# Rewriting a linear-attention and mixture-of-experts kernel: decay before the transposes, state in PSUM, small matmuls for the sums, one load queue, a fixed order

One core of one Trainium2 chip. The metric is the time of one execution in device microseconds (us); lower is better. A slow run is over 1.5% above the fastest of its kernel; comparisons below use fast runs.

## The reference, cut to what matters

```python
# attention, per batch b (4) and head h (8), head size 48, 768 steps
for t in range(S):
    cur = einsum('bhd,bhe->bhde', u * kt, vt)
    y[:, :, t] = einsum('bhd,bhde->bhe', rt, state + cur)
    state = w * state + einsum('bhd,bhe->bhde', kt, vt)
# mixture of experts, one expert per batch (sentence)
e_idx = argmax(x.mean(axis=1) @ w_gate)          # x: (4, 768, 384)
out[b] = gate[b] * (relu(x[b] @ w1[e]) @ w2[e])  # w1 (8, 384, 1024), w2 (8, 1024, 384)
```

The kernels cut each batch into 6 chunks of 128 steps, so there are 24 chunks. Inside a chunk the recurrence becomes masked matmuls; between chunks a state is carried. An expert can be chosen only when its batch's six chunks are done, so the expert of batch b runs beside the chunks of batch b+1, and the last one runs alone.

## The kernel before

```python
    # loads of one chunk (r, k in f32 by SyncE; v cast to bf16 by a POOL-issued transfer)
    nc.sync.dma_start(out=rr32[:, :, 0:D], in_=r[b, :, s0 : s0 + C, :].transpose([1, 0, 2]))
    nc.sync.dma_start(out=kk32[:, :, 0:D], in_=k[b, :, s0 : s0 + C, :].transpose([1, 0, 2]))
    nc.gpsimd.dma_start(out=vv, in_=v[b, :, s0 : s0 + C, :].transpose([1, 0, 2]))
    nc.gpsimd.memset(rr32[:, :, D:DP], 0.0)
    nc.gpsimd.memset(kk32[:, :, D:DP], 0.0)
    nc.scalar.copy(rr, rr32)
    nc.scalar.copy(kk, kk32)
    # one chunk
    nc.gpsimd.tensor_mul(ku, kk[:, :, 0:D], u_bc)           # bonus
    nc.gpsimd.tensor_mul(rku, rr[:, :, 0:D], ku)
    nc.vector.reduce_sum(tcol, rku, axis=AX.X)
    nc.gpsimd.tensor_mul(kr, kk, wr)                        # decay for the state
    # ... 8 transposes into PSUM twp ...
    nc.vector.tensor_mul(tw, twp, dcT)                      # decay after the transposes
    # ... scores into atp, twice:
    nc.vector.tensor_mul(gt[:, 4 * wave : 4 * wave + 4, :], atp, maskT)
    # ... y matmuls; 8 state matmuls into kvp ...
    nc.gpsimd.tensor_mul(stmp[0:D], st[0:D, :, 0:D], wCst[0:D])
    nc.gpsimd.tensor_mul(stmp[64 : 64 + D], st[64 : 64 + D, :, D:96], wCst[64 : 64 + D])
    nc.vector.tensor_add(st[0:D, :, 0:D], stmp[0:D], kvp[0:D, :, 0:D])
    # ... and the other half ...
    nc.gpsimd.tensor_mul(vt, vv, tcol.to_broadcast([128, H, D]))
    nc.vector.tensor_add(xn, vt, yp)
    # ... transposes back; eviction with a running sum for the gate ...
```

Of the kernel before, what the change touches and what calls it, by code (L numbers as in the profile page):

```python
# [18 lines left out]
def kernel(  # L19
# [26 lines left out]
    NST = S // 128  # L46

    const = ctx.enter_context(tc.tile_pool(name="const", bufs=1))
    work = ctx.enter_context(tc.tile_pool(name="work", bufs=3))
    inpool = ctx.enter_context(tc.tile_pool(name="inpool", bufs=6))  # L50
    trans = ctx.enter_context(tc.tile_pool(name="trans", bufs=2))
    xpool = ctx.enter_context(tc.tile_pool(name="xpool", bufs=2))
    spool = ctx.enter_context(tc.tile_pool(name="spool", bufs=2))
    wpool = ctx.enter_context(tc.tile_pool(name="wpool", bufs=2))
    hpool = ctx.enter_context(tc.tile_pool(name="hpool", bufs=1))
    opool = ctx.enter_context(tc.tile_pool(name="opool", bufs=3))
    gpool = ctx.enter_context(tc.tile_pool(name="gpool", bufs=2))

    pp_tw = ctx.enter_context(tc.tile_pool(name="pp_tw", bufs=1, space=bass.MemoryType.PSUM))
    pp_at = ctx.enter_context(tc.tile_pool(name="pp_at", bufs=2, space=bass.MemoryType.PSUM))  # L60
    pp_y = ctx.enter_context(tc.tile_pool(name="pp_y", bufs=2, space=bass.MemoryType.PSUM))
    pp_kv = ctx.enter_context(tc.tile_pool(name="pp_kv", bufs=1, space=bass.MemoryType.PSUM))
    pp_moe = ctx.enter_context(tc.tile_pool(name="pp_moe", bufs=2, space=bass.MemoryType.PSUM))

    ident = const.tile([128, 128], BF16, tag="ident", name="ident")
# [4 lines left out]
    )  # L70

# [7 lines left out]
    w_flat = w.rearrange("h d -> (h d)")  # L79
    u_flat = u.rearrange("h d -> (h d)")  # L80
    wbc = const.tile([128, H, D], FP32, tag="wbc", name="wbc")
    nc.sync.dma_start(out=wbc, in_=w_flat.partition_broadcast(128))
    lnw = const.tile([128, H, D], FP32, tag="lnw", name="lnw")
    nc.scalar.activation(out=lnw, in_=wbc, func=ACT.Ln)

    u_bc = const.tile([128, H, D], BF16, tag="u_bc", name="u_bc")
    nc.gpsimd.dma_start(out=u_bc, in_=u_flat.partition_broadcast(128))

    idx_col = const.tile([128, 1], FP32, tag="idx_col", name="idx_col")
    nc.gpsimd.iota(idx_col, pattern=[[0, 1]], base=0, channel_multiplier=1,  # L90
                   allow_small_or_imprecise_dtypes=True)
    idxr_col = const.tile([128, 1], FP32, tag="idxr_col", name="idxr_col")
    nc.gpsimd.iota(idxr_col, pattern=[[0, 1]], base=C - 1, channel_multiplier=-1,
                   allow_small_or_imprecise_dtypes=True)

    scratch = const.tile([128, H, D], FP32, tag="scratch", name="scratch")

    wr = const.tile([128, H, DP], BF16, tag="wr", name="wr")
    nc.vector.memset(wr, 0.0)
    nc.vector.tensor_scalar_mul(scratch, in0=lnw, scalar1=idxr_col[:, 0:1])  # L100
    nc.scalar.activation(out=wr[:, :, 0:D], in_=scratch, func=ACT.Exp)

    wTcol = const.tile([128, NP], FP32, tag="wTcol", name="wTcol")
    nc.vector.memset(wTcol, 1.0)
    for p in range(NP):
        nc.sync.dma_start(out=wTcol[0:D, p : p + 1], in_=w[2 * p, :].rearrange("d -> d ()"))
        nc.sync.dma_start(out=wTcol[64 : 64 + D, p : p + 1], in_=w[2 * p + 1, :].rearrange("d -> d ()"))
    lnwT = const.tile([128, NP], FP32, tag="lnwT", name="lnwT")
    nc.scalar.activation(out=lnwT, in_=wTcol, func=ACT.Ln)

    iota_row = const.tile([128, 128], FP32, tag="iota_row", name="iota_row")
    nc.gpsimd.iota(iota_row, pattern=[[1, 128]], base=0, channel_multiplier=0,
                   allow_small_or_imprecise_dtypes=True)

    dcT = const.tile([128, 2 * NP, 128], BF16, tag="dcT", name="dcT")
    nc.vector.memset(dcT, 0.0)
    scrT = const.tile([128, 128], FP32, tag="scrT", name="scrT")
    for p in range(NP):
        nc.vector.tensor_scalar_mul(scrT, in0=iota_row, scalar1=lnwT[:, p : p + 1])
        for lo, hi in ((0, D), (64, 64 + D)):  # L120
            nc.scalar.activation(out=dcT[lo:hi, p, :], in_=scrT[lo:hi], func=ACT.Exp)
        nc.vector.tensor_scalar(
            out=scrT, in0=iota_row, scalar1=lnwT[:, p : p + 1], scalar2=lnwT[:, p : p + 1],
            op0=ALU.mult, op1=ALU.add,
        )
        for lo, hi in ((0, D), (64, 64 + D)):
            nc.scalar.activation(out=dcT[lo:hi, NP + p, :], in_=scrT[lo:hi], func=ACT.Exp, scale=-1.0)

    wCst = const.tile([128, NP, D], BF16, tag="wCst", name="wCst")
    nc.vector.memset(wCst, 0.0)  # L130
    scrC = const.tile([128, NP], FP32, tag="scrC", name="scrC")
    nc.scalar.activation(out=scrC, in_=lnwT, func=ACT.Exp, scale=float(C))
    nc.vector.tensor_copy(wCst, scrC.to_broadcast([128, NP, D]))

    wg = const.tile([128, NCT, E], FP32, tag="wg", name="wg")
    nc.sync.dma_start(out=wg, in_=moe_w_gate.rearrange("(ct p) e -> p ct e", p=128))
    nc.scalar.mul(wg, wg, 1.0 / float(S))

    ones_row = const.tile([1, 128], FP32, tag="ones_row", name="ones_row")
    nc.vector.memset(ones_row, 1.0)  # L140

    def alloc_batch_tiles(b):
        xt = xpool.tile([128, NCT, S], BF16, tag="xt", name=f"xt{b}")
        st = spool.tile([128, NP, 96], BF16, tag="st", name=f"st{b}")
        nc.vector.memset(st, 0.0)
        pooled_acc = spool.tile([128, NCT], FP32, tag="pooled_acc", name=f"pooled_acc{b}")
        nc.vector.memset(pooled_acc, 0.0)
        return xt, st, pooled_acc

    def load_chunk(b, ci):  # L150
        s0 = ci * C
        rr32 = inpool.tile([128, H, DP], FP32, tag="rr32", name="rr32")
        kk32 = inpool.tile([128, H, DP], FP32, tag="kk32", name="kk32")
        vv = inpool.tile([128, H, D], BF16, tag="vv", name="vv")
        nc.sync.dma_start(out=rr32[:, :, 0:D], in_=r[b, :, s0 : s0 + C, :].transpose([1, 0, 2]))
        nc.sync.dma_start(out=kk32[:, :, 0:D], in_=k[b, :, s0 : s0 + C, :].transpose([1, 0, 2]))
        nc.gpsimd.dma_start(out=vv, in_=v[b, :, s0 : s0 + C, :].transpose([1, 0, 2]))  # L157
        nc.gpsimd.memset(rr32[:, :, D:DP], 0.0)  # L158
        nc.gpsimd.memset(kk32[:, :, D:DP], 0.0)
        rr = inpool.tile([128, H, DP], BF16, tag="rr", name="rr")  # L160
        kk = inpool.tile([128, H, DP], BF16, tag="kk", name="kk")
        nc.scalar.copy(rr, rr32)  # L162
        nc.scalar.copy(kk, kk32)  # L163
        return rr, kk, vv

    def rwkv_chunk(b, ci, xt, st, pooled_acc, loaded):
        s0 = ci * C
        first = ci == 0
        last = ci == NCH - 1
        rr, kk, vv = loaded  # L170

        ku = work.tile([128, H, D], BF16, tag="ku", name="ku")
        rku = work.tile([128, H, D], BF16, tag="rku", name="rku")
        tcol = work.tile([128, H], BF16, tag="tcol", name="tcol")
        nc.gpsimd.tensor_mul(ku, kk[:, :, 0:D], u_bc)  # L175
        nc.gpsimd.tensor_mul(rku, rr[:, :, 0:D], ku)  # L176
        with nc.allow_low_precision("bonus coefficients are small"):
            nc.vector.reduce_sum(tcol, rku, axis=AX.X)  # L178
        kr = work.tile([128, H, DP], BF16, tag="kr", name="kr")
        nc.gpsimd.tensor_mul(kr, kk, wr)  # L180

        twp = pp_tw.tile([128, 2 * NP, 128], BF16, tag="tw", name="twp")
        for p in range(NP):
            nc.tensor.transpose(  # L184
                out=twp[:, p, :],
                in_=rr[:, 2 * p : 2 * p + 2, :].rearrange("s a b -> s (a b)"),
                identity=ident,
            )
            nc.tensor.transpose(  # L189
                out=twp[:, NP + p, :],  # L190
                in_=kk[:, 2 * p : 2 * p + 2, :].rearrange("s a b -> s (a b)"),
                identity=ident,
            )
        tw = trans.tile([128, 2 * NP, 128], BF16, tag="tw", name="tw")
        nc.vector.tensor_mul(tw, twp, dcT)  # L195

        gt = trans.tile([128, H, 128], BF16, tag="gt", name="gt")
# [148 lines left out]
    def emit_moe_jobs(n):  # L346
        for _ in range(n):
            if moe_jobs:
                moe_jobs.pop(0)()
# [76 lines left out]
```

## Time and profile before

| | before |
|---|---|
| median of 3 runs | 227.76 us (227.17 to 228.2) |
| busy: PE, DVE, ACT, POOL | 141.0, 113.1, 92.6, 170.9 us |
| loads of r, k (SyncE), v (POOL), 192 bytes a piece | 4.1, 3.9, 4.1 us from issue to landing |

The engines: PE is TensorE (PEld its weight loads), DVE VectorE, ACT ScalarE, POOL GpSimd, SP SyncE. The page's summary of the chain that ended last, followed back from the last instruction, gives shares of the span by engine:

```profile
POOL 41%; PE 20%; DMA 12%; issue 10%; DVE 8%; ACT 4%; SPq 2%; POOLq 1%; ACTq 0%; DVEq 0%
```

POOL holds most of that chain.

### The profile page before, as it was taken

How to read it: one execution, taken by the hardware profiler on the slowest of the kernel's cores; microseconds unless marked ns; L12 is line 12 of the kernel's file. 1: busy time of each engine (PE TensorE's matmuls, PEld its weight loads, DVE VectorE, ACT ScalarE, POOL GpSimd, SP SyncE). 2: the span in 40 equal slices, each digit the busy share in tenths (PEclk: the TensorE clock that was granted, in tenths of full speed). 3: DMA queues.
4: the chain of work that ended last, by engine and by line, in shares of the span. 5: the costliest groups of instructions: out<-in, count | busy, mean ns of one | idle time of the engine just before them, and what ended most of it. 6: DMA issues, size and time to landing. Idle time of an engine off the chain costs nothing.

```text
span 227.5 us, 3977 instructions
## 1 busy us (share of the span) xinstructions
PE 141.0 (62%) x1304; PEld 83.5 (37%) x1304; DVE 113.1 (50%) x255; ACT 92.6 (41%) x291; POOL 170.9 (75%) x276
## 2 busy tenths in 40 slices
PE   0020275534552896375996139289895899967993
PEld 0010154423341463142554015155552454533461
DVE  2153297655775369426773055287893564101200
ACT  3585544332521263235453214306343266325542
POOL 8469999999999989999999899996795601920000
PEclk9999999999999999975599956959999699999998
DMA  4999999877968997480379940333089320995022
GB/s 56 139 192 198 197 209 166 117 85 86 123 89 111 142 162 55 47 129 1 17 91 226 173 52 0 20 17 18 10 115 215 82 72 0 125 211 152 0 102 106
DMA packets 87620, 23.37 MB, mean 103 GB/s; under 512 B 77104, under 2 KB 87600, under 8 KB 87600
## 3 DMA queue, kind: packets, MB, share of 16 engines
q0 software_dynamic: 33168, 8.75, 39.9%
q1 hardware_dynamic: 54432, 14.37, 29.3%
q8 instruction: 10, 0.16, 0.3%
q14 instruction: 10, 0.08, 0.1%
HBM read 27.15 MB, written 4.72 MB: 140 GB/s over the span
## 4 chain that ended last, share of the span: by engine, by line
POOL 41%; PE 20%; DMA 12%; issue 10%; DVE 8%; ACT 4%; SPq 2%; POOLq 1%; ACTq 0%; DVEq 0%
PE hp L317 9%; POOL rku L176 7%; POOL kr L180 7%; DMA w<-in_moe_w_dram 7%; PE op L332 6%; POOL ku L175 6%; POOL vt L252 6%; POOL vv L157 6%; POOL stmp L245 3%; DMA rr<-in_r_dram 3%; DMA out_dram<-ob 3%; POOL stmp L244 2%; DVE xn L254 1%; DVE gt L211 1%; ACT ht L325 1%
## 5 line engine op out<-in xcount | busy, mean ns | idle before, releaser
L317 PE MATMUL hp<-xt,w 128*128 128x384 bf16 x192 | 47.3, 365 | 14.8 <-ACT ht L325 6.8
L332 PE MATMUL op<-w,ht 128*128 128x384 bf16 x192 | 37.8, 341 | 2.3 <-ACT ob L340 1.8
L211 DVE TENSOR_TENSOR gt<-atp,maskT 128x512 bf16<-128x512 f32 x48 | 31.3, 683 | 11.6 <-PE atp L204 11.5
L264 ACT ACTIVATE xt<-xtp 128x128 bf16<-128x128 bf16 x72 | 19.0, 274 | 37.5 <-PE xtp L259 33.3
L325 ACT ACTIVATE ht<-hp 128x384 bf16<-128x384 f32 x48 | 23.1, 491 | 25.1 <-PE hp L317 24.9
L180 POOL TENSOR_TENSOR kr<-kk,wr 128x512 bf16<-128x512 bf16 x24 | 27.6, 1148 | 1.7 <-PE kvp L236 1.4
L317 PEld LDWEIGHTS <-w 128*128 128x128 bf16 x192 | 18.1, 104 | 28.5 <-issue 16.7
L184 PE MATMUL twp<-ident,rr 128*128 128x128 bf16 x96 | 20.1, 271 | 11.8 <-ACT rr L162 11.8
L340 ACT ACTIVATE ob<-op,gate_bc 128x384 f32<-128x384 f32 x24 | 13.9, 581 | 32.5 <-PE op L332 13.3
L175 POOL TENSOR_TENSOR ku<-kk,u_bc 128x384 bf16<-128x384 bf16 x24 | 21.6, 901 | 4.8 <-ACT kk L163 4.8
L178 DVE TENSOR_REDUCE tcol<-rku 128x8 bf16<-128x384 bf16 x24 | 13.0, 546 | 22.0 <-POOL rku L176 17.7
L306 POOL DMA_DIRECT2D w<-in_moe_w_dram x24 | 13.3, 559 | 13.8 <-DVE gate_bc L297 13.6
L332 PEld LDWEIGHTS <-ht 128*128 128x128 bf16 x192 | 17.9, 101 | 14.1 <-issue 4.7
L157 POOL DMA_DIRECT2D vv<-in_v_dram x24 | 22.4, 935 | 0.7 <-PE hp L317 0.6
L215 PE MATMUL yp<-vv,gt 128*128 128x48 bf16 x192 | 14.2, 202 | 12.9 <-DVE gt L211 12.7
L204 PE MATMUL atp<-tw 48*128 48x128 bf16 x192 | 12.9, 271 | 14.9 <-DVE tw L195 14.3
L176 POOL TENSOR_TENSOR rku<-rr,ku 128x384 bf16<-128x384 bf16 x24 | 21.7, 905 | 0.3
L162 ACT CAST rr<-rr 128x512 bf16<-128x512 f32 x24 | 14.9, 621 | 15.5 <-POOL rr L158 11.3
L252 POOL TENSOR_TENSOR vt<-vv,tcol 128x384 bf16<-128x384 bf16 x24 | 19.9, 828 | 1.2 <-DVE xn L254 0.6
L311 POOL DMA_DIRECT2D w<-in_moe_w_dram x32 | 17.2, 558 | 4.6 <-issue 2.6
L189 PE MATMUL twp<-ident,kk 128*128 128x128 bf16 x96 | 20.1, 272 | 0.9 <-ACT kk L163 0.9
L327 DVE TENSOR_SCALAR ht<-hp 128x384 bf16<-128x384 f32 x16 | 8.7, 551 | 20.3 <-PE hp L317 20.2
(66 smaller groups left out, 231.0 us busy)
## 6 DMA issues: line engine op xcount, KB each, us to landing
rr<-in_r_dram SPq DMA_DIRECT2D x24, 192.0 KB, 4.1
kk<-in_k_dram SPq DMA_DIRECT2D x24, 192.0 KB, 3.9
out_dram<-ob SPq DMA_DIRECT2D x24, 192.0 KB, 3.3
w<-in_moe_w_dram POOLq DMA_DIRECT2D x24, 128.0 KB, 4.2
w<-in_moe_w_dram POOLq DMA_DIRECT2D x32, 96.0 KB, 5.7
vv<-in_v_dram POOLq DMA_DIRECT2D x24, 96.0 KB, 4.1
wbc<-in_w_dram SPq DMA_DIRECT2D x1, 192.0 KB, 3.3
wTcol<-in_w_dram SPq DMA_DIRECT2D x8, 0.2 KB, 2.7
```

The lines of the kernel that those rows point to most:

```text
L157: nc.gpsimd.dma_start(out=vv, in_=v[b, :, s0 : s0 + C, :].transpose([1, 0, 2]))
L175: nc.gpsimd.tensor_mul(ku, kk[:, :, 0:D], u_bc)
L176: nc.gpsimd.tensor_mul(rku, rr[:, :, 0:D], ku)
L180: nc.gpsimd.tensor_mul(kr, kk, wr)
L184: nc.tensor.transpose(out=twp[:, p, :], in_=rr[:, 2 * p : 2 * p + 2, :].rearrange("s a b -> s (a b)"), identity=ident,)
L189: nc.tensor.transpose(out=twp[:, NP + p, :], in_=kk[:, 2 * p : 2 * p + 2, :].rearrange("s a b -> s (a b)"), identity=ident,)
L211: nc.vector.tensor_mul(gt[:, 4 * wave : 4 * wave + 4, :], atp, maskT)
L252: nc.gpsimd.tensor_mul(vt, vv, tcol.to_broadcast([128, H, D]))
L264: nc.scalar.activation(out=xt[:, ct, s0 : s0 + C], in_=xtp[:, ct, :], func=ACT.Copy, accum_out=psum_part[:, ct : ct + 1])
L317: nc.tensor.matmul(out=hp, lhsT=w1[:, ct, 128 * ft : 128 * (ft + 1)], rhs=xt[:, ct, SB * sb : SB * (sb + 1)], start=(ct == 0), stop=(ct == ...
L325: nc.scalar.activation(out=ht[:, ft, SB * sb : SB * (sb + 1)], in_=hp, func=ACT.Relu)
L332: nc.tensor.matmul(out=op, lhsT=ht[:, ft, 128 * si : 128 * (si + 1)], rhs=w2[:, ft, :], start=(ft == 0), stop=(ft == NFT - 1),)
```

## The change

The intent: take elementwise work off POOL. The decay goes onto k and r before the transposes (two POOL products per chunk, written as bf16, with a shared midpoint over groups of three chunks). The state is then a plain sum that PE accumulates in PSUM, the bonus and the pooled mean become small matmuls, all loads go through SyncE, and every engine gets a fixed order with expert jobs placed between the steps of a chunk. The core of the diff, with cuts at "...":

```diff
+    AHEAD = 8
-    opool = ctx.enter_context(tc.tile_pool(name="opool", bufs=3))
+    opool = ctx.enter_context(tc.tile_pool(name="opool", bufs=4))
+    ctx.enter_context(tc.manual_schedule())
...
+        for name, src in (("k32", k), ("r32", r), ("v32", v)):
+            nc.sync.dma_start(out=t, in_=src[b, :, s0 : s0 + C, :].transpose([1, 0, 2]))
...
-        nc.gpsimd.tensor_mul(ku, kk[:, :, 0:D], u_bc)
-        nc.gpsimd.tensor_mul(rku, rr[:, :, 0:D], ku)
-        nc.gpsimd.tensor_mul(kr, kk, wr)
+        nc.gpsimd.tensor_mul(kp[i][:, :, 0:D], k32, dk[:, m])
+        nc.gpsimd.tensor_mul(rp[i][:, :, 0:D], r32, dr[:, m])
+        nc.gpsimd.tensor_copy(vb, v32)
...
-        nc.vector.tensor_mul(tw, twp, dcT)
+        nc.scalar.copy(tw, twp)
+        nc.vector.tensor_mul(prod, tw[:, 0:NP, :], tw[:, NP : 2 * NP, :])   # bonus: 4 matmuls with U8
...
-        nc.vector.tensor_add(st[0:D, :, 0:D], stmp[0:D], kvp[0:D, :, 0:D])
+        # 4 matmuls add into PSUM sp over the chunks
+        nc.vector.tensor_mul(st, sp[...], msk)
...
+    for n in range(N):
+        if n + AHEAD < N: load(n + AHEAD)
+        if n + 2 < N: prep(n + 2)
+        if b and ci == 0: weights(b - 1)
+        if n + 1 < N: transposes(n + 1)
+        moe(q); outputs(n); state(n); moe(q)
+        if n + 1 < N: pa = scores(n + 1)
+        backs(n); moe(q)
+        if n + 1 < N: bonus(n + 1, *pa)
+        moe(q)
+        if ci == NCH - 1: gate(b)
+        moe(q)
+    weights(B - 1)
+    moe(len(jobs))
```

## The prediction

> **What bounds the kernel now.** I read four views in this order: the busy times, a table by stage, the costliest groups, and the chain that ended last in the tail.
>
> ```profile
> PE 141.0 (62%) x1304; PEld 83.5 (37%) x1304; DVE 113.1 (50%) x255; ACT 92.6 (41%) x291; POOL 170.9 (75%) x276
> ...
> 14.00:60.00 46.00, 19.73 (x236) 14.24 (x236) 27.86 (x52) 20.79 (x64) 45.06 (x70) 1.00 0.98 149
> 60.00:100.00 40.00, 25.12 (x252) 15.48 (x252) 25.64 (x54) 14.42 (x51) 38.70 (x61) 0.96 0.86 108
> 100.00:165.00 65.00, 43.76 (x430) 25.05 (x429) 36.91 (x90) 24.14 (x88) 59.54 (x89) 0.79 0.48 59
> 165.00:200.00 35.00, 31.16 (x269) 17.21 (x268) 17.28 (x43) 15.22 (x53) 18.17 (x33) 0.95 0.60 101
> 200.00:228.00 28.00, 19.98 (x113) 10.76 (x111) 2.07 (x4) 10.98 (x21) 0.99 (x2) 0.97 0.43 113
> ```
>
> The first line gives each engine's share. The others are stretches, with busy us in the order PE, PEld, DVE, ACT, POOL, then granted clock, DMA share and GB/s. POOL's 75% hides two regimes: from 14 to 165 us it is busy 143.3 of 151 us, and after 165 it falls away. So for two thirds of the span the kernel is bound by POOL: 24 chunks (4 batches of 6) at about 170.9/24 = 7.1 us of POOL each. PE, DVE and ACT have 5.9, 4.7 and 3.9 us per chunk. The POOL groups:
>
> ```profile
> L180 POOL TENSOR_TENSOR kr<-kk,wr 128x512 bf16<-128x512 bf16 x24 | 27.6, 1148 | 1.7 <-PE kvp L236 1.4
> ...
> L175 POOL TENSOR_TENSOR ku<-kk,u_bc 128x384 bf16<-128x384 bf16 x24 | 21.6, 901 | 4.8 <-ACT kk L163 4.8
> ...
> L157 POOL DMA_DIRECT2D vv<-in_v_dram x24 | 22.4, 935 | 0.7 <-PE hp L317 0.6
> ...
> L252 POOL TENSOR_TENSOR vt<-vv,tcol 128x384 bf16<-128x384 bf16 x24 | 19.9, 828 | 1.2 <-DVE xn L254 0.6
> ```
>
> With rku (905 ns), two stmp (545 each), two memsets and the expert-weight issues (56 at 0.56 us) this is the whole of it. After 165 us the last batch's expert is exposed; two pieces of the chain carry it:
>
> ```profile
> 208.88 0.66 PE hp L317 x3
> ...
> 215.86 7.82 PE op L332 x48
> ```
>
> The first expert matmul runs in 16 groups of 3, one pair of groups per 1.23 us (two PSUM buffers, each waiting for its Relu); the second is 48 matmuls at 7.82/48 = 0.163 us. Then 0.58 us of eviction and about 3.1 us of store.
>
> **What the Trainium skill says.** (1) "GPSIMD Engine Reference", section 3.1: a two-input elementwise op costs about 2.6 cycles per element at 1.2 GHz, measured in f32; section 4.1: one input is roughly line rate. The trace gives (1148-901)/128 = 1.93 ns per element, 2.3 cycles, in bf16: near enough that I take 0.92 us for an f32 product of 384. No copy by POOL is in the trace; my estimate from the page is 384/1.2 GHz plus about 0.16 us = 0.5 us. (2) "VectorE: DVE Perf Modes", the perf-mode tier table: a bf16 tensor_tensor in SBUF runs at 2x, one with PSUM at 1x. The trace agrees for the f32 PSUM mask product (512 elements, 683 ns = 512/0.96 GHz + 150) but not for the bf16 PSUM product tw, whose 1024 elements also take 681 ns, so 2x. (3) "ScalarE: Activation LUTs", section "What ACT_TABLE_LOAD costs": about 1283 ns a load, 186 ns + 0.833 ns per element an ACTIVATE, and 93 ns more with a pointer operand. The trace has 1283 ns, and 581 against 491 ns for ob with and ht without the pointer. (4) "TensorE: Matmul & The Clock Gate", Part 1: a 128-column matmul starts every 107 ns cold and 56 ns warm. The trace has both: transposes start 0.107 us apart at 13 us and 0.055 apart at 142 us.
>
> **The change part by part.** POOL loses ku, rku, kr, stmp, the memsets and the v issues, and gains two f32 products (k and r times decay, into bf16) and a copy of v. Per chunk: 2 x 0.92 + 0.5 + vt 0.83 = 3.2 us, where it had 7.1. Weight issues fall from 14 to 2 per batch. POOL total about 24 x 3.2 + 10 = 87 us: it stops being the bound.
>
> DVE loses the tcol reduce (0.55), tw (0.68), two st adds (0.70) and the pooled add (0.55). It gains prod (512 bf16 in SBUF at 2x: 256/0.96 + 150 = 0.42), a small tcol copy (0.17) and st as one 384-element PSUM product (0.55). With two gt at 0.683 and xn at 0.55 it is 3.05 us per chunk. Of the expert it takes a third of the Relus and half of the obs, 0.55 us each: 8 per 28 jobs.
>
> ACT loses both casts and the accumulating evictions (9 small instructions become one copy of 384, about 0.5 us). It gains the copy of tw, 186 + 0.833 x 1024 = 1.04 us. That is 1.55 us per chunk, plus the expert's share, about 1.3 us per 5 jobs.
>
> PE keeps the transposes and scores, has 4 state matmuls for 8, and gains 4 bonus and 3 pooled ones with 8 and 1 columns. Warm, by the pitches above: transposes 0.45, scores 0.25, y 0.35, state 0.17, back 0.25, bonus 0.1, with waits about 1.7 us. The fixed order places 5 expert jobs in each chunk from the tenth on: per 28 jobs 16 of 0.49 us (three matmuls) and 12 of 0.65 (four), so 5 cost 2.8 us.
>
> Timeline. Start: the decay broadcast lands at 4.2 us as now; Ln to 4.7, table load to 6.0, six Exp of 0.6 us to 9.2, the first tw copy to 10.4. Then two more table loads with two small activations, to 13.4: the second tw copy and DVE's wcmask wait for them. I put the second chunk's prod at 15.5 us. Without expert jobs the loop is DVE's 3.05 us plus a bubble, because xn waits for the y matmuls that wait for the last gt: 0.06 us signal, about 0.8 cold, 0.1 back. Loop 4.0 us; 8 chunks 32; one gate 2.5: 50 us. With jobs, PE needs 1.7 + 2.8 = 4.5 and DVE 3.05 + 0.8 + bubble, 4.6; since both go in fixed order and wait for each other I take 5.0. 15 chunks 75, two gates 5: 130 us. Tail: gate chain 3, register load 1.3 (from the index at 161.9 to the issue at 163.2 in the trace), issue 1, first weights 5.5 (786 KB at the 215 GB/s that the slices reach, plus landing): 11 us, under which the 9 jobs left over (6 us) hide. Then 16 x 0.613 = 9.9, 1 for a cold start, 7.8, and 4.2 for eviction and store: 34. Sum 164 us.
>
> DMA: loads are now 73,728 packets of 192 bytes. On the hardware queue the page's share gives 0.293 x 16 x 227.5/54,432 = 19.6 ns per packet and engine, 3.8 us per chunk at worst; the early slices at 197 GB/s, where a chunk was 393 KB of r and k and 98 KB of v landed as bf16, give 491/197 = 2.5 us. Either is under 4.0; what the weights add to it is rival (c).
>
> **The rivals.** (a) POOL stays the bound, because f32 products cost twice bf16 ones: 4 x 0.92 + 1.33 = 5.0 per chunk, so 8 more early and about 5 later, 177 us. For it: no f32 product by POOL is in the trace. Against: the skill's own f32 figure. (b) The fixed order serialises: y, tw, state and xn each have one PSUM buffer, the jobs two, and one late DVE eviction holds PE and everything behind it. If the loops become 4.8 and 6.5 us: 6 + 22 more, 192 us. For it: the groups of this kernel already wait for Relus, and five engines of near equal load rarely interlock perfectly. Against: the jobs lie exactly where PE would wait. (c) The load queue becomes the bound: loads run 8 chunks ahead, so the last one is issued in the sixteenth of 24 chunks, at about 85 us. Up to there 24 chunks at 3.8 are 91 us, with two experts' weights 16 more (1.57 MB each at 197 GB/s): 107 in place of 85, and as the last chunks then have slack again perhaps 15 of the 22 stay: 179. Against: at the 2.5 us that the early slices carried it is 60 + 16 = 76, which fits. (d) Better: both loops at DVE's floor (3.7 and 4.4), 9 us less, 153.
>
> **Range and chances.** 164 us; the rivals spread from 153 to 192 and (b) is the likeliest, so 149 to 183. All of them stay far below 223, since taking 4 us of POOL off each chunk has no engine ready to take its place: faster 0.96, same 0.02, slower 0.02.
>
> **What would show it.** POOL near 87 us busy and kp at 0.9 us; DVE near 95 and the chain led by DVE and PE, not POOL; a chunk every 4 us before 50 us and every 5 after; four table loads; wcmask ending near 14 us; the last expert starting about 11 us after the last gate began. Wrong if kp takes 1.5 us or more, if chunks take over 6 us with PE idle behind waits for gt or evictions, or if prep waits for loads.

## The result, and the profile after

| | before | after |
|---|---|---|
| median of the runs | 227.98 us (227.17 to 231.59, 4 runs, the last one slow) | 174.37 us (173.69 to 177.94, 4 runs, one of them slow) |
| ratio, fast runs | | 0.7629, 95% interval 0.758 to 0.7678 |

A ratio here compares the fast runs of both kernels, so it is not quite the ratio of the medians quoted (the means of the fast runs in this table give 0.765).

The page's busy times, chain and costliest groups of the kernel after:

```profile
PE 131.3 (76%) x1392; PEld 88.9 (52%) x1392; DVE 91.5 (53%) x227; ACT 73.5 (43%) x121; POOL 87.8 (51%) x114
...
PE 48%; DVE 18%; DMA 12%; issue 5%; SPq 5%; POOL 4%; ACT 4%; POOLq 0%; DVEq 0%; ACTq 0%
...
L184 POOL TENSOR_TENSOR kp<-k,dk 128x384 bf16<-128x384 f32 x24 | 23.9, 997 | 4.2 <-ACT dk L128 4.2
...
L208 DVE TENSOR_TENSOR prod<-tw 128x512 bf16<-128x512 bf16 x24 | 14.2, 590 | 2.2 <-ACT tw L202 2.2
L187 POOL CAST vb<-v 128x384 bf16<-128x384 f32 x24 | 13.8, 575 | 0.0
```

POOL has half the work it had and has nearly left the chain (41% to 4%); PE and DVE lead. The same table by stage as before the change, cut where the stages of this kernel change (chunks without expert jobs from 18.5 to 50.5, with them to 138.6, the last expert after that; columns as in the prediction's table):

```profile
18.50:50.50 32.00, 26.10 (x335) 22.26 (x332) 24.85 (x56) 12.12 (x17) 27.75 (x34) 1.00 1.18 185
50.50:78.00 27.50, 26.16 (x304) 17.39 (x303) 19.83 (x49) 14.03 (x25) 19.44 (x25) 1.00 1.15 188
78.00:90.50 12.50, 2.98 (x43) 2.00 (x40) 0.05 (x2) 1.34 (x2) 2.74 (x4) 0.69 1.13 204
90.50:138.60 48.10, 45.17 (x520) 29.33 (x520) 32.89 (x77) 25.68 (x45) 25.92 (x32) 0.94 0.54 109
138.60:172.50 33.90, 25.94 (x142) 14.36 (x142) 7.01 (x19) 9.19 (x18) 1.71 (x2) 0.94 0.50 117
```

The third row stands out. In 12.5 us DVE is busy for 0.05 and PE for 2.98, while the transfers move 204 GB/s. DVE stops first, and the other engines soon after it. The list of waits (total, times, longest, in us) names the wait:

```profile
DVE ob L390 <- DMA out_dram<-ob: 12.4, 1, 12.4
```

`ob` is the output tile of the expert. There are four, and the fifth eviction of a batch must wait for the store of the first. The timeline of the SyncE queue shows why that store was late (columns: start, duration, engine):

```profile
70.74 0.95 SPq L81 DMA_DIRECT2D v<-in_v_dram  x1
71.78 5.45 SPq L81 DMA_DIRECT2D k<-in_k_dram  x1
77.32 4.21 SPq L81 DMA_DIRECT2D r<-in_r_dram  x1
81.63 1.86 SPq L81 DMA_DIRECT2D v<-in_v_dram  x1
83.58 1.53 SPq L81 DMA_DIRECT2D k<-in_k_dram  x1
85.21 0.85 SPq L81 DMA_DIRECT2D r<-in_r_dram  x1
86.15 0.69 SPq L81 DMA_DIRECT2D v<-in_v_dram  x1
86.93 1.27 SPq L391 DMA_DIRECT2D out_dram<-ob  x2
```

The first tile was evicted at 71.92 us, but its store stands behind six loads in SyncE's order. The second expert's weights were issued by POOL at 69.7 and 70.5 us; from then on a load takes up to 5.45 us to issue in place of about 0.95. The store leaves at 86.93, lands 3.4 us later, and DVE goes on at 90.45. The Trainium skill, "Trainium Kernel Development and Optimization", section "Key Constraints", says that transfers issued from the SP, ACT and POOL queues run on the same 16 DMA engines and interleave. The trace agrees: SyncE's loads slow down while POOL's transfer runs, here and after the first weights (issued at 42.7 us, loads then take up to 4.03 us to issue).

Two smaller departures are visible. First, prod takes 590 ns on average where 420 was predicted. The timeline (start, duration) shows when:

```profile
25.58 1.00 POOL L185 TENSOR_TENSOR rp<-r,dr 128x384 bf16<-128x384 f32 x1
25.91 0.95 DVE L208 TENSOR_TENSOR prod<-tw 128x512 bf16<-128x512 bf16 x1
26.52 0.71 POOL L187 CAST vb<-v 128x384 bf16<-128x384 f32 x1
```

A prod that starts inside a POOL product ends 0.28 us after that product's end, and the copy behind it takes 0.71 us where it takes 0.50 alone; a prod beside an idle POOL takes 0.41. "SBUF — State Buffer", section "SBUF: two separate sides", has this: a DVE operation with two SBUF inputs and a GpSimd operation that reads SBUF share one pair of ports as an exclusive lock. I had not applied it. Second, the start is late: the transposes of the first chunk begin at 11.67 us, behind a broadcast of u that lands at 8.8 us and is the fifth transfer on SyncE.

### The profile page after: what moved, and what is told of

Same layout as the page of the kernel before. It is cut to its first block, busy times and chain, and to the rows that moved or that the text cites. A ratio compares the mean times of both kernels' runs of the same rounds, so it can differ in the third digit from the quotient of the medians.

```text
span 172.5 us, 3663 instructions
## 1 busy us (share of the span) xinstructions
PE 131.3 (76%) x1392; PEld 88.9 (52%) x1392; DVE 91.5 (53%) x227; ACT 73.5 (43%) x121; POOL 87.8 (51%) x114
## 4 chain that ended last, share of the span: by engine, by line
PE 48%; DVE 18%; DMA 12%; issue 5%; SPq 5%; POOL 4%; ACT 4%; POOLq 0%; DVEq 0%; ACTq 0%
PE hp L365 16%; PE op L381 13%; PE twp L196 7%; SPq L81 5%; DVE prod L208 5%; DMA w<-in_moe_w_dram 5%; DVE xn L255 3%; DVE ht L374 3%; DMA ubc<-in_u_dram 3%; DMA v<-in_v_dram 2%; DVE st L281 2%; PE y L250 2%; PE y L245 2%; DMA out_dram<-ob 2%; PE xp L297 2%
## 5 line engine op out<-in xcount | busy, mean ns | idle before, releaser
L236 POOL TENSOR_TENSOR vt<-vb,tcol 128x384 bf16<-128x384 bf16 x24 | 19.9, 830 | 42.6 <-DVE tcol L233 42.6
L202 ACT COPY tw<-twp 128x1024 bf16<-128x1024 bf16 x24 | 24.3, 1011 | 17.9 <-PE twp L196 17.8
L184 POOL TENSOR_TENSOR kp<-k,dk 128x384 bf16<-128x384 f32 x24 | 23.9, 997 | 4.2 <-ACT dk L128 4.2
L365 PEld LDWEIGHTS <-w 128*128 128x128 bf16 x192 | 17.4, 103 | 15.5 <-issue 5.9
L185 POOL TENSOR_TENSOR rp<-r,dr 128x384 bf16<-128x384 f32 x24 | 24.4, 1019 | 0.0
L255 DVE TENSOR_TENSOR xn<-vt,y 128x384 bf16<-128x384 bf16 x24 | 13.2, 551 | 16.2 <-PE y L250 15.2
L390 DVE TENSOR_SCALAR ob<-op,gw 128x384 f32<-128x384 f32 x12 | 7.4, 616 | 24.2 <-DMA out_dram<-ob 12.4
L297 PE MATMUL xp<-ident,xn 128*128 128x128 bf16 x72 | 9.8, 257 | 10.9 <-DVE xn L255 10.9
L220 DVE TENSOR_TENSOR gt<-at,maskT 128x512 bf16<-128x512 f32 x24 | 16.4, 682 | 0.6 <-PE at L212 0.6
L234 DVE TENSOR_TENSOR gt<-at,maskT 128x512 bf16<-128x512 f32 x24 | 16.2, 677 | 0.0
L208 DVE TENSOR_TENSOR prod<-tw 128x512 bf16<-128x512 bf16 x24 | 14.2, 590 | 2.2 <-ACT tw L202 2.2
L187 POOL CAST vb<-v 128x384 bf16<-128x384 f32 x24 | 13.8, 575 | 0.0
L196 PE MATMUL twp<-ident,kp 128*128 128x128 bf16 x96 | 11.7, 261 | 1.5 <-DVE U L160 1.5
L196 PE MATMUL twp<-ident,rp 128*128 128x128 bf16 x96 | 12.2, 266 | 0.0
## 6 DMA issues: line engine op xcount, KB each, us to landing
w<-in_moe_w_dram POOLq DMA_DIRECT2D x8, 768.0 KB, 10.9
```

The costliest lines, as they stand in the source:

```text
L184: nc.gpsimd.tensor_mul(kp[i][:, :, 0:D], k32, dk[:, m])
L185: nc.gpsimd.tensor_mul(rp[i][:, :, 0:D], r32, dr[:, m])
L196: nc.tensor.transpose(out=twp[:, o + p, :], in_=src[:, 2 * p : 2 * p + 2, :].rearrange("s a b -> s (a b)"), identity=ident,)
L202: nc.scalar.copy(tw, twp)
L208: nc.vector.tensor_mul(prod, tw[:, 0:NP, :], tw[:, NP : 2 * NP, :])
L220: nc.vector.tensor_mul(gt[:, 0], at[0], maskT)
```

## The experiments

Theory Q: the difference between 164 and 174 us is the store that stands behind loads, with four output tiles. Rival D: the transfers are the bound, and any time won at that wait comes back as waits for loads. All kernels gave correct results. Each was timed beside the kernel before in its own rounds (medians of before: 229.22, 229.53 and 229.59 us), and the ratio is to that. The changed kernel itself was not timed again in these rounds: its 174.37 us is from the first one, where before was 227.98.

| run | edit | median us | ratio to before, 95% interval |
|---|---|---|---|
| e1_ob8 | 8 output tiles | 162.67 | 0.71, 0.7051 to 0.7149 |
| e2_store_act | stores by ScalarE, 4 tiles | 170.37 | 0.7439, 0.7389 to 0.7489 |
| e3_ahead11 | loads 11 ahead, 4 tiles | 186.51 | 0.8116, 0.803 to 0.8201 |
| b1_kr_dve | kernel before, kr by DVE | 203.45 | 0.8898, 0.8837 to 0.8958 |
| e4_ob8_scheduler | e1 without the fixed order | 170.42 | 0.7435, 0.7388 to 0.7482 |
| e6_prod_psum | e1, prod from PSUM | 157.82 | 0.6886, 0.6835 to 0.6936 |
| e7_ubc_act | e1, u by ScalarE | 160.18 | 0.7007, 0.6967 to 0.7047 |
| e8_tail | e1, split fetch, 4 PSUM tiles | 157.67 | 0.6893, 0.6854 to 0.6932 |
| e9_all | e1, e6, e7, e8 together | 155.17 | 0.6774, 0.6729 to 0.6819 |
| e10_all_ahead12 | e9, loads 12 ahead | fast runs 154.77 and 156.92 | none given |

**More output tiles.**

```diff
-    opool = ctx.enter_context(tc.tile_pool(name="opool", bufs=4))
+    opool = ctx.enter_context(tc.tile_pool(name="opool", bufs=8))
```

> The changed kernel with 8 output tiles in place of 4, nothing else. Theory Q (queue order): the one 12.45 us idle of VectorE at 78 us is the fifth output eviction waiting for a free output tile, because the first store stands on the SyncE queue behind input loads that crawl while the expert weights are moved; with 8 tiles for the 6 evictions of a batch nobody waits: 162 to 166 us, and the idle in front of that eviction is gone from the list of waits. Rival D (transfers are the bound): all 16 DMA engines are full until 98 us, so what is saved at that wait comes back as waits of the POOL products for their loads: 170 to 175 us.

Measured 162.67 us, 11.7 less than the changed kernel's 174.37. The wait is gone from the list. The stores themselves leave no earlier (the first at 89.2 us); nobody waits for them any more. The stage of chunks with expert jobs, in the table by stage of this version:

```profile
51.00:127.00 76.00, 72.30 (x862) 47.55 (x859) 52.97 (x127) 40.97 (x71) 48.18 (x60) 0.96 0.92 173
```

It takes 76.0 us where the changed kernel took 88.1, and PE is busy for 95% of it. POOL now waits for loads three times, 3.5 us in sum (1.6 at most), where the changed kernel's list has no such wait; this is far from 12. Theory Q holds; rival D fails here.

**Stores by another engine.**

```diff
-            nc.sync.dma_start(out=out[b, 128 * si : 128 * si + 128, :], in_=ob)
+            nc.scalar.dma_start(out=out[b, 128 * si : 128 * si + 128, :], in_=ob)
```

> The changed kernel with the stores issued by ScalarE in place of SyncE, still 4 output tiles. Theory Q: the stores no longer stand behind loads, the tile comes free about 4 us after its eviction: 162 to 167 us. Rival D: 170 to 175 us, with POOL waiting for loads.

Measured 170.37 us: a gain of 4, not of 10. The first three stores do leave within 2 us of their evictions. The fourth does not, and ScalarE stands still behind it. The chain that ended last, then ScalarE's timeline:

```profile
70.20 15.48 DMA k<-in_k_dram
```

```profile
85.76 0.34 ACTq L391 DMA_DIRECT2D out_dram<-ob  x1
86.14 1.01 ACT L202 COPY tw<-twp 128x1024 bf16<-128x1024 bf16 x1 [7.91 <-DMA k<-in_k_dram]
```

A store waits for a k load (that of chunk 18) that has nothing to do with it. The program built from this kernel says why: loads and stores share eight completion semaphores (DMAHW0 to DMAHW7), and each transfer first waits for the last user of its own. Two of its instructions, shortened:

```
SP   L81  DMACopy k_18_1047<-in_k_dram   [waits DMAHW4_49,Pool_49]
ACT  L391 DMACopy out_dram<-ob_3_1465    [waits DMAHW4_49,Activation_49]
```

The store waits until the semaphore has counted 128, which is the count that this k load completes. So another queue does not free the stores: by the shared semaphore they still wait for slow loads, and now hold ScalarE. The size in my expectation was wrong; that the stores hang on the loads was right.

**More loads ahead.**

```diff
-    AHEAD = 8
+    AHEAD = 11
```

> The changed kernel with loads 11 chunks ahead in place of 8 (12 input buffers). In the program the first store then stands behind the last load instead of three loads before it. Theory Q: the store leaves only when all loads have been issued, so the wait grows from 12.45 us to 16 to 20: 178 to 183 us. Rival D, or the plain view that more prefetch helps: loads come earlier, 168 to 174 us.

Measured 186.51 us, 12 slower than the changed kernel. This goes the way of theory Q and against the plain view that more prefetch helps, and further than I wrote. In the list of waits and on the SyncE timeline:

```profile
DVE ob L390 <- DMA out_dram<-ob: 24.8, 1, 24.8
```

```profile
98.31 8.00 SPq L391 DMA_DIRECT2D out_dram<-ob  x6
```

The stores leave only after the last load, as the program orders them, and the wait doubles from 12.4 to 24.8 us.

**The bound of the kernel before.**

```diff
-        nc.gpsimd.tensor_mul(kr, kk, wr)
+        nc.vector.tensor_mul(kr, kk, wr)
```

> The kernel before with one POOL operation per chunk (kr, 1.148 us) done by VectorE instead. If POOL was the bound of the 24 chunks, as predicted, 1.15 us less per chunk is worth up to 27 us, less what VectorE's order costs: 203 to 212 us. If POOL only looked full and the waits between engines or the transfers set the pace, the time stays within 2% of 228.

Measured 203.45 against 229.22 us: 25.8 less, of at most 24 x 1.148 = 27.6. POOL's busy time fell from 170.9 to 146.1 us, as the page's busy times show. Nearly all of the work taken from POOL came off the time, so POOL was the bound.

```profile
PE 135.4 (67%) x1304; PEld 81.8 (41%) x1304; DVE 115.0 (57%) x279; ACT 92.3 (46%) x291; POOL 146.1 (72%) x252
```

One line did half as much as the whole rewrite did at first (53 us).

**Without the fixed order.**

```diff
-    ctx.enter_context(tc.manual_schedule())
```

> The version with 8 output tiles, with the fixed order taken away: the scheduler of the language orders each engine's instructions itself (all of them move). If the gain comes from the lighter POOL and DVE work, whatever the order, it stays within 5 us of 162.7. If the fixed interleaving of expert jobs into chunks matters, jobs and chunks bunch up, PE waits for evictions, and it takes 170 to 190 us.

Measured 170.42 us, 7.7 more than e1 and at the near edge of the second case. The busy times are like e1's (POOL 88.7, DVE 95.8). In the list of waits:

```profile
POOL w L347 <- DVE gw L337: 11.7, 4, 5.3
...
PE hp L364 <- DMA w<-in_moe_w_dram: 8.0, 2, 4.5
```

The first expert's weights are issued at 47.8 us in place of 43.3, POOL stands idle for the gate in all four batches, 11.7 us in sum (in e1 once, 6.6 us), and PE waits twice for weights instead of once (8.0 against 3.7 us). Most of the gain is lighter work; the order adds 7.7 us. How these waits divide the 7.7 was not separated.

**prod with one operand from PSUM.**

```diff
-        nc.vector.tensor_mul(prod, tw[:, 0:NP, :], tw[:, NP : 2 * NP, :])
+        nc.vector.tensor_mul(prod, tw[:, 0:NP, :], twps.pop(n)[:, NP : 2 * NP, :])
```

> The version with 8 output tiles, and prod reading its second operand from PSUM (the transposes) in place of SBUF (their copy). In the changed kernel prod took 590 ns on average against 420 predicted: 0.41 where POOL stood idle, 0.85 to 1.2 where POOL was in a two-input product. Theory S (both read SBUF through a shared interface): with one SBUF operand prod takes 410 to 450 ns throughout, and the nine chunks without expert jobs get 0.3 to 0.5 us shorter each: 158.5 to 161 us in all. Rival (prod is slow for another reason, such as its dependence on the copy): it stays near 590 ns, 162 to 163.5 us. Third: prod gets short but the loads set the pace, so 162 us all the same, with POOL waiting for loads.

Measured 157.82 us, 4.8 less than e1, slightly better than the range (one of the six runs is slow; the five fast ones have a mean of 157.41). The profile fell in the run marked slow, so I use only durations and the distances of early chunks from it:

```profile
L209 DVE TENSOR_TENSOR prod<-tw,twp 128x512 bf16<-128x512 bf16 x24 | 9.9, 411 | 2.2 <-ACT tw L202 2.2
```

From 590 to 411 ns on average, with a maximum of 422 (1220 in the changed kernel). Only the place of one operand changed, so reading both from SBUF was the cause. That it is GpSimd which this collides with is shown from the other side: POOL's copy vb, which was not touched, fell from 559 ns on average in e1 to 515. Early chunks went from 3.84 to about 3.3 us, where POOL's own 3.2 to 3.4 is close.

**u by another queue at the start.**

```diff
-    nc.sync.dma_start(out=ubc, in_=u...)
+    nc.scalar.dma_start(out=ubc, in_=u...)
```

> The version with 8 output tiles, and the broadcast of u issued by ScalarE at the start in place of SyncE after the first three loads. If the late start (first transposes at 11.67 us, where the products were ready at about 9.0) comes from this load (landed at 8.8 us), as I read it, the first transposes begin at 9.0 to 9.3 us and everything is 2 to 2.7 us earlier: 159.5 to 161 us. If the start is bound by the decay products or by the loads, 162 to 163 us.

Measured 160.18 us, 2.5 less than e1. In the timeline the first transposes now wait for POOL's product alone, and start at 9.85 us. This is later than the 9.0 to 9.3 I wrote: beside the broadcast of u the one of the decay now lands later (ScalarE's Ln starts at 6.21 us, where it started at 4.50), and with it the products.

```profile
9.85 0.61 PE L196 MATMUL twp<-ident,kp 128*128 128x128 bf16 x4 [2.17 <-POOL kp L184]
```

**The tail.**

```diff
+        for f0 in range(0, F, F // 2):          # w1 in two halves of its columns
-        hp = pp_moe.tile(...)
+        hp = pp_at.tile(...) if tail and (ft * NSB + sb) % 2 else pp_moe.tile(...)
```

> The version with 8 output tiles; each first expert weight fetched in two halves of its columns, and in the last expert the first matmul's groups take two more PSUM tiles (free by then) in turn. The tail from the last gate to the end was 33.9 us, of which the fetch held 11.1 and the 16 groups 11.3 at 0.6 to 0.7 us apart. Expected: fetch of the first half 2 us shorter, groups 0.5 us apart (8.0 in all): 156.5 to 159.5 us. If the fetch is bound by the stores and the second half that share it, and the groups by ScalarE's Relus, 161 to 163 us.

Measured 157.67 us, 5.0 less than e1. The trace divides it: from the start of the last gate to the first group takes 9.1 us (11.3 in e1), from there to the second matmul 8.2 (11.1 in e1). Both came as expected. But the chain that ended last shows a limit I had not named:

```profile
132.00 12.61 DMA w<-in_moe_w_dram
144.65 7.99 PE op L387 x48
```

The second weight lands 12.6 us after its issue, and the second matmul waits 0.2 us for it: the groups of the first matmul now end just before this transfer does, so faster groups alone would gain nothing more. The two edits were not run apart.

**All together.**

> All of these together: 8 output tiles, prod from PSUM, u by ScalarE, split fetch and four PSUM tiles at the end. If the gains lie in separate stages they add: 151 to 155 us. If the loads become the bound once chunks are shorter (all 16 engines were full until 98 us), a part of it is lost and POOL waits for loads: 155 to 159 us.

Measured 155.17 us: 0.6774 of before. The three gains over e1 sum to 4.8 + 2.5 + 5.0 = 12.3 us; 7.5 came. The trace shows a new wait of about the size of the missing 4.8: POOL waits for a load, and DVE idles once for 4.68 us (the bracket in the second fence; PE's expert group stood behind the transposes of that chunk).

```profile
POOL rp L185 <- DMA r<-in_r_dram: 3.0, 1, 3.0
```

```profile
56.06 0.56 DVE L381 TENSOR_SCALAR ht<-hp 128x384 bf16<-128x384 f32 x1 [4.68 <-PE hp L372]
```

That r load was issued at 39.72 us and landed 13.6 us later, while the first expert's weights were moved. With early chunks at 3.1 to 3.3 us in place of 3.84, a part of rival D comes true.

**More lead for that.** The edit is AHEAD = 12 on top of e9.

> All four improvements, with loads 12 chunks ahead in place of 8. In the version with 8, the r load of the twelfth chunk took 13.6 us from issue to landing while the first expert's weights were moved, POOL waited 3.0 us for it and VectorE idled 4.7 us. Theory D (the DMA engines are full from the start, so lead cannot grow): no change, 154 to 156.5 us, the same wait. Rival (the loads are issued too late because of the buffer count): the wait disappears, 150 to 152 us.

Of four timed runs two were fast (154.77 and 156.92 us) and two slow (162.31 and 163.31). Theory D had 154 to 156.5: one fast run lies there, the other (the profiled one) just above. Two waits for loads are left in it, and a wait that e9 did not have:

```profile
POOL kp L184 <- DMA k<-in_k_dram: 3.8, 1, 3.8
POOL rp L185 <- DMA r<-in_r_dram: 1.5, 1, 1.5
```

```profile
DVE ob L397 <- DMA out_dram<-ob: 4.0, 2, 3.8
```

More buffers do not bring the loads earlier: the k load of the twelfth chunk is issued at 38.77 us, in e9 at 38.68. But the run is no clean test of the time. With 12 chunks of lead the stores leave only after the last load (98.11 us, in e9 88.27), 8 output tiles no longer suffice for the next expert, and the wait of theory Q is back. Just before it this run is 0.5 us ahead of e9, at its end 1.6 behind. What the lead is worth with enough output tiles was not run.

## Why the prediction was right or wrong

It was right: 174.37 us lies in 149 to 183, and faster was given 0.96. The direction and its reason hold: POOL was the bound, and no engine took its place at 7.1 us per chunk (b1 and the busy times). The range was met although it had no term for the largest departure, one wait of 12.45 us. The sum of 164 is that of a span; the profiled run's time of 174.17 us is 1.7 above its span of 172.5, which the sum left out. Term by term, with that span:

| term | predicted | measured |
|---|---|---|
| start, to the second chunk's prod | 15.5 | 18.5 |
| 8 chunks without jobs and one gate | 34.5 | 32.0 |
| 15 chunks with jobs and two gates | 80 | 88.1 (76.0 in e1) |
| tail from the last gate | 34 | 33.9 |
| POOL busy | 87 | 87.8 |
| DVE busy | near 95 | 91.5 |

Without the wait (e1) it is 162.67 us, next to the 164 predicted. That is partly luck: the late start and the 1.7 us outside the span were made up by chunks that were faster than predicted.

- **Start: 3 us too short.** I started the first transposes from the decay products alone and left out that the u constant must be transposed before them. e7 gave 2.5 us back. wcmask ended at 17.6 us, not near 14, mostly for the same reason; the four table loads were there as said.
- **Chunks without jobs: 3.84 us against 4.0, but by two errors that cancel.** prod cost 0.4 to 0.5 us more, because of the ports shared with POOL. Against that, DVE instructions follow each other 0.07 to 0.09 us sooner than their durations say, and the bubble before xn was 0.68 us in place of 0.96.
- **Chunks with jobs: the term that failed.** The 5.0 us per chunk was sound: without the wait, 15 chunks and two gates take 76.0 us, 4 less than predicted. What failed is that I looked at the DMA engines' rate and at compute orders, but not at what stands in front of a store on the load queue. Rival (b) said that "one late DVE eviction holds PE and everything behind it"; that is what happened, but from a PSUM or job buffer I expected it, not from an output tile. Rival (c) had the loads falling behind, and put the cost on the compute that waits for them; in fact the cost fell on the stores queued behind them (e1, e3). A sign of this stood in the list of waits before the change, where evictions waited four times for one of the three output tiles:

```profile
ACT ob L340 <- DMA out_dram<-ob: 7.0, 4, 3.1
```

- **Tail: right in sum.** From the start of the last gate to the first group took 11.1 us (predicted 11), the groups 11.3 (10.9 with the cold start), the second matmul 7.9 and the end 3.6 (4.2). The 5.5 us for the first weights was wrong in itself: 8.0, while the gate and register load took less.
- **The f32 products.** 1.0 us in place of 0.92, and 0.575 for the copy: rival (a) did not come about. The 0.92 leaned on the pace of the bf16 products (1.93 ns per element); from 1.0 us, with the same 0.16 us of fixed cost, the f32 pace is 2.18 ns.
- **A sign of the shared ports** may also have been there before the change: the pooled add has two SBUF inputs and only 3 elements, and took 150 to 1684 ns. I took its mean of 0.55 us for its cost. Whether POOL caused this was not tested.
- **Sums and readings.** In rival (d), 8 x 0.3 and 15 x 0.6 are 11.4 us less, not 9; the 153 is right. 16 x 0.613 is 9.8, not 9.9. In the DMA part, the 2.5 us per chunk counted v as landed in bf16, but the changed kernel lands f32: 590 KB at 197 GB/s are 3.0. SyncE issued a chunk of loads every 3.06 us from 26 to 41 us, and the last load of all at 97.1 us, between the 76 and the 107 of rival (c).

What stays open: why a load crawls so much while weights are moved (the rate of all transfers together does not fall), how e4's waits divide the 7.7 us, and what more lead is worth with enough output tiles.

## What to carry to other kernels

When an engine's work is halved, look next at the in-order queues: for each buffer that is freed by a transfer, count what stands in front of that transfer and how slow it can get when something large shares the DMA engines. A few more output tiles cost nothing here and were worth 12 us, where more prefetch made things worse. The count holds for one lead only: with 12 chunks of lead, 8 tiles were too few again (e10). And before giving VectorE an operation with two SBUF inputs beside a busy GpSimd, see whether one of them can be read from PSUM.

## What the Trainium skill lacked or had wrong

- "VectorE: DVE Perf Modes", perf-mode tier table: it puts tensor_tensor with any PSUM operand at 1x (the text below the table, "Why PSUM operands drop a tier", allows 2x for 16-bit types). With bf16 in PSUM it ran at 2x: 681 ns for 1024 elements in the kernel before, and 411 ns for 512 with one operand in PSUM in e6.
- "SBUF — State Buffer", section "SBUF: two separate sides": the lock is as the runs show it, but no page gives its cost for a short product beside a GpSimd product. Here a 512-element product went from 0.41 to 0.95 us (1.22 at most), and the POOL copy behind it from 0.50 to 0.71.
- "GPSIMD Engine Reference", sections 3.1 and 4.1: no figure at this size for an f32 product written as bf16 (997 ns for 384 elements; section 3.1's 2.6 cycles per element, with the 0.16 us of fixed cost that this case's bf16 products leave, give an estimate of 0.99 us) or an f32 to bf16 copy (575 ns on average, 0.50 us alone).
- None that I read has it: the issue of a load by SyncE can itself take 5.45 us (7.82 in e2), where 0.95 is usual, while a POOL-issued transfer of expert weights runs; what follows in that queue waits as long.
